# A chunked mLSTM mixer and its MLP on one core: the output gates get tiles of their own, F and g share one 128-row tile, w1's third rows are copied by DMA, and the plan has new numbers

## The chip, the core and the metric

The kernel runs on one core of a Trainium2 chip. Its metric is the device time in microseconds (us). Before the change the median of three runs is 384.98 us (384.32 to 384.99). The engines are TensorE (PE, its weight loads PEld), VectorE (DVE), ScalarE (ACT), GpSimd (POOL) and SyncE (SP), which issues nearly all DMAs.

## The reference

The first part is an mLSTM over 768 steps, for 4 batches of 8 heads of width 40; the second mixes the tokens of its output by a product of rank 32 and applies an MLP of width 320 to 1280 to 320.

```python
for t in range(S):                       # per batch and head
    m_new = max(f[t] + m, i[t])
    C = exp(f[t] + m - m_new) * C + exp(i[t] - m_new) * outer(v[t], k[t])
    n = exp(f[t] + m - m_new) * n + exp(i[t] - m_new) * k[t]
    m = m_new
    y[t] = sigmoid(o[t]) * (C @ q[t]) / max(abs(n . q[t]), 1.0)
x = y, heads side by side                # 4 x 768 x 320
u = x + (x^T @ U @ V)^T                  # mixes tokens
out = u + max(u @ w1, 0) @ w2
```

## The kernel before

The steps are cut into chunks of 128 tokens, three to a half (hf), two halves to a batch; the eight heads go in groups of 3, 3 and 2. For a half, the gates of all 32 batch-head rows are worked out at once (function gates): a running maximum (gate_max, L525), some differences, the running sum F of the log decays within a chunk (gate_sum, L534, the rows fs), and g = exp(F) (gate_exp). For each head, TensorE spreads F over 128 partitions (decay, function fbmm), ScalarE takes exp(F + a bias per token) in three pieces (decay_exp, L923), GpSimd masks the upper triangle (decay_mask, L926), VectorE multiplies with the scores of q and k (weigh, L937), and TensorE multiplies with V (pv). A group's state C is carried by kv, kv_mask and state; inter adds its part from q times g (q_decay, from g_rows for batch 0 and from a DMA for later batches). norm, out_norm and gate (L964 to L977) divide, multiply by the sigmoid of the output gate and write x. Batches 2 and 3 (from LOG_TO = 2) build the decays by a scan on VectorE (L933) from DMAs instead of exponentials on ScalarE.

TensorE's products in reduced form take each operand as a high part plus a low part (the names _high and _low): F and g are split so into the tiles fhl and ghl. fhl has four 32-row strips, F high, F low, F high, F low; a decay matmul uses 64 rows, so that two heads go as a pair on the two 64-row halves of the array. The weights come as 64-bit words, which ScalarE and VectorE turn into 32-bit floats (L649 to L654) and split; w1's third rows (64 of 320) are written to both halves of w1h's third strip (w13_high, L721).

The token tile tk of a group holds K, V and the output gates o of its three chunks. The sigmoid is taken in place (L773), for batches 0 and 1 three groups at a time (most = 3), for later ones singly. The sigmoid and the exponential use different tables of ScalarE.

The order of the work is not written by hand. Each operation is given to a planner (class Plan) with an engine or a choice of engines, a cost in ns, its reads and writes, the buffers it opens, and a priority: a due time plus a number from the table ORDER, by kind of operation and by half of a batch. The planner goes through simulated time, starts on each engine the ready operation of the smallest priority, and emits the instructions in this order; each engine's queue then runs in it, and so does SP's queue of DMAs. Operations that wait for a table of ScalarE's other than the one loaded get a penalty (SWITCH). PSUM's 8 banks are shared by the kinds st, at, m1, m2 and gt with a limit for each (SHARE). Where TensorE would be idle, or its use in a stretch of time too low, the planner emits fillers: matmuls of a zero tile into a free bank (keep_busy, warm). attention, mix and mlp give the planner the operations of a batch; the MLP of a half is 10 strips of up (eight matmuls of 384 columns each), relu and down (three times three matmuls of 320 columns).

Of the kernel before, what the change touches and what calls it, by code (L numbers as in the profile page):

```python
# [45 lines left out]
G_TO, QUAD_FROM = 1, 2  # L46
MASK_NS = 600.0
# [24 lines left out]
    "gate_w": (87.18, 86.38, 0.0, 0.0, 0.0, 0.0, 0.0, 0.0),
    "gate_exp": (96.46, 1090.3, 0.0, 0.0, 0.0, 0.0, 0.0, 0.0),
    "gate_w_exp": (82.17, 121.49, 0.0, 0.0, 0.0, 0.0, 0.0, 0.0),
    "store_g": (89.27, 82.16, 0.0, 0.0, 0.0, 0.0, 0.0, 0.0),
    "g_high": (823.51, 82.38, 0.0, 0.0, 0.0, 0.0, 0.0, 0.0),
    "g_low": (43.02, 90.34, 0.0, 0.0, 0.0, 0.0, 0.0, 0.0),
    "gate_f_exp": (44.34, 953.57, 0.0, 0.0, 0.0, 0.0, 0.0, 0.0),
    "gate_ends": (68.95, 85.66, 0.0, 0.0, 0.0, 0.0, 0.0, 0.0),
    "gate_i_exp": (72.57, 90.34, 0.0, 0.0, 0.0, 0.0, 0.0, 0.0),  # L80
    "store_decay": (67.79, 88.08, 0.0, 0.0, 0.0, 0.0, 0.0, 0.0),
    "gate_turn": (77.56, 86.18, 0.0, 0.0, 0.0, 0.0, 0.0, 0.0),
    "gate_keep": (75.92, 90.34, 0.0, 0.0, 0.0, 0.0, 0.0, 0.0),
    "gate_total": (44.17, 111.25, 0.0, 0.0, 0.0, 0.0, 0.0, 0.0),
    "totals": (66.83, 173.14, 0.0, 0.0, 0.0, 0.0, 0.0, 0.0),
    "totals_keep": (74.35, 104.22, 0.0, 0.0, 0.0, 0.0, 0.0, 0.0),
    "load_weights": (-8.4, 0.0, 0.0, 0.0, 0.0, 0.0, 0.0, 0.0),
# [1151 lines left out]
```

## Time and profile before

| | |
|---|---|
| profiled execution | 385.04 us |
| its span (first to last instruction) | 383.2 us |
| TensorE busy | 375.7 us, 98% |
| VectorE busy | 246.9 us, 64% |
| ScalarE busy | 164.8 us, 43% |
| GpSimd busy | 44.8 us, 12% |
| granted TensorE clock | 0.998 of 2.4 GHz |
| moved by DMA | 47.25 MB |

A share of the span is an average over stages that differ, and a matmul is counted as busy until its modelled end, which overlaps the next one's start: 12 matmuls that are listed at 285 ns each may hold the queue for under 1 us. What an operation holds of TensorE's queue is read from the start of the one behind it.

### The profile page before, as it was taken

To read this page: it belongs to the slowest core of one execution; us is meant where nothing else is said; L and a number is where in the kernel's file an instruction comes from. 1 tells how busy PE (TensorE), PEld (TensorE's weight loads), DVE (VectorE), ACT (ScalarE), POOL (GpSimd) and SP (SyncE) were. 2 spreads that over 40 slices of the span, in tenths; PEclk is the share of its full clock that TensorE was granted. 3 is DMA by queue.
4 is the path that set the end of the run, shared out by engine and by line. 5 is a ranking of instruction groups with operands and counts; after the bars stand their busy time and mean duration, and the time that the engine had idled before them with its cause. 6 is when DMAs were issued, how large, how long until landed. Compare 5 with 4: busy or idle time off the path is not lost.

```text
span 383.2 us, 7435 instructions
## 1 busy us (share of the span) xinstructions
PE 375.7 (98%) x2776; PEld 355.0 (93%) x2776; DVE 246.9 (64%) x562; ACT 164.8 (43%) x411; POOL 44.8 (12%) x68
## 2 busy tenths in 40 slices
PE   8999999999999999999999999999999999999996
PEld 6687877889999999999999999999999999999996
DVE  4977989989988857554498554888935334213222
ACT  6897697985976422132223142313222122213120
POOL 0123344223113300020010000002000000000000
PEclk9999999999999999999999999999999999999999
DMA  8958999576725732156276341553201000000001
GB/s 192 351 177 237 274 246 256 169 202 186 226 84 154 213 89 85 58 130 199 71 185 185 80 136 51 133 153 110 85 19 36 0 2 18 33 2 19 34 1 53
DMA packets 26052, 47.25 MB, mean 123 GB/s; under 512 B 4192, under 2 KB 17120, under 8 KB 26016
## 3 DMA queue, kind: packets, MB, share of 16 engines
q1 hardware_dynamic: 25824, 46.38, 42.2%
q8 instruction: 22, 0.36, 0.4%
q10 hardware_dynamic: 192, 0.40, 0.3%
q14 instruction: 14, 0.11, 0.1%
HBM read 41.85 MB, written 4.92 MB: 122 GB/s over the span
## 4 chain that ended last, share of the span: by engine, by line
PE 83%; DVE 7%; DMA 5%; ACT 2%; issue 2%; ACTq 0%; SPq 0%; DVEq 0%
PE ps L402 83%; DMA tk<-in_tk 2%; DMA q<-in_q 2%; DMA x<-in_fig 1%; DVE cv L654 1%; DVE cv L652 1%; DVE dm L937 1%; DVE w1l L699 0%; DVE w1l L723 0%; DVE fhl L546 0%; ACT dm L923 0%; DVE cv L650 0%; ACT L923 0%; ACT L1128 0%; ACT fhl L543 0%
## 5 line engine op out<-in xcount | busy, mean ns | idle before, releaser
L402 PE MATMUL ps<-w2h,h 128*128 128x320 f32 x480 | 118.8, 312 | 0.0
L402 PE MATMUL ps<-ut,w1h 128*128 128x384 f32 x400 | 117.9, 342 | 0.0
L1092 DVE SCALAR_TENSOR_TENSOR h<-ps,h 128x384 fp32r<-128x384 f32 x80 | 44.0, 552 | 77.1 <-ACT h L1090 76.8
L1090 ACT ACTIVATE h<-ps 128x384 fp32r<-128x384 f32 x80 | 39.0, 491 | 114.2 <-PE ps L402 114.2
L402 PEld LDWEIGHTS ps<-w2h,h 128*128 128x128 f32 x480 | 83.2, 188 | 0.7 <-issue 0.4
L402 PE MATMUL ps<-ut,w1l 128*128 128x384 f32 x240 | 80.6, 336 | 0.0
L402 PEld LDWEIGHTS ps<-ut,w1h 128*128 128x128 f32 x400 | 73.6, 188 | 1.4 <-issue 0.3
L402 PE MATMUL ps<-w2l,h 128*128 128x320 f32 x240 | 73.9, 308 | 0.0
L402 PE MATMUL ps<-tk,dm 128*128 128x82 f32 x384 | 49.9, 272 | 0.3 <-DVE dm L937 0.3
L402 PEld LDWEIGHTS ps<-tk,dm 128*128 128x128 f32 x384 | 47.3, 191 | 2.8 <-DVE dm L937 1.3
L402 PEld LDWEIGHTS ps<-ut,w1l 128*128 128x128 f32 x240 | 45.1, 188 | 0.0
L402 PEld LDWEIGHTS ps<-w2l,h 128*128 128x128 f32 x240 | 45.1, 188 | 0.0
L937 DVE TENSOR_TENSOR dm<-ps,dm 128x384 f32<-128x384 f32 x64 | 33.4, 545 | 5.2 <-PE ps L402 2.9
L933 DVE TENSOR_TENSOR_SCAN dm<-fd,ident 128x384 f32<-128x384 f32 x32 | 30.5, 960 | 5.1 <-DMA fd<-fsd 3.7
L923 ACT ACTIVATE dm<-ps,tok 128x128 f32<-128x128 f32 x96 | 26.9, 371 | 4.5 <-PE ps L402 4.4
L402 PE MATMUL ps<-qk 40*128 40x128 f32 x384 | 28.3, 285 | 0.0
L402 PEld LDWEIGHTS ps<-qk 40*128 40x128 f32 x384 | 23.6, 187 | 4.8 <-issue 3.3
L402 PE MATMUL ps<-zeros 128*128 128x256 bf16 x172 | 25.9, 294 | 2.0 <-DVE x L522 1.1
L926 POOL TENSOR_SCALAR_AFFINE_SELECT dm<-dm 128x384 f32<-128x384 f32 x32 | 18.9, 594 | 69.2 <-ACT dm L923 64.3
L402 PEld LDWEIGHTS <-zeros 128*128 128x128 bf16 x172 | 17.0, 106 | 6.8 <-issue 1.8
L1115 DVE TENSOR_TENSOR o<-ps,x 128x320 f32<-128x320 f32 x24 | 10.9, 487 | 9.9 <-PE ps L402 9.9
L402 PE MATMUL ps<-C,q 120*128 120x123 f32 (+1 forms) x120 | 17.2, 277 | 0.0
(101 smaller groups left out, 418.3 us busy)
## 6 DMA issues: line engine op xcount, KB each, us to landing
qk<-in_qk SPq DMA_DIRECT2D x64, 144.0 KB, 3.5
tk<-in_tk SPq DMA_DIRECT2D x16, 544.5 KB, 6.2
raw<-in_w SPq DMA_DIRECT2D x20, 320.0 KB, 4.1
fd<-fsd SPq DMA_DIRECT2D x32, 192.0 KB, 3.3
out<-o SPq DMA_DIRECT2D x24, 160.0 KB, 1.8
tk<-in_tk SPq DMA_DIRECT2D x8, 363.0 KB, 5.3
q<-in_q SPq DMA_DIRECT2D x16, 180.0 KB, 2.5
fd<-gsd SPq DMA_DIRECT2D x9, 120.0 KB, 3.8
```

What stands on the lines that cost most here:

```text
L402: nc.tensor.matmul(o, a, b, start=start, stop=stop, **kw)
L652: p.op("weight_sign" + at, pri, "dve", dve(n), lambda tu=tu, hi=hi: V.scalar_tensor_tensor(tu(), hi(), 0x80000000, tu(), ALU.bitwise_and, ...
L654: p.op("weight_tail" + at, pri, "dve", dve(n), lambda tu=tu, lo=lo: V.scalar_tensor_tensor(tu(), lo(), 29, tu(), ALU.logical_shift_right, ...
L923: nc.scalar.activation(T[kdm][:, cs], T[kfb][:, cs], AF.Exp, bias=tok[hf][:, 0, c, bh:bh + 1])
L926: p.op("decay_mask", at(u), "pool", MASK_NS, lambda kdm=kdm: nc.gpsimd.affine_select(out=T[kdm].rearrange("p (c t) -> p c t", t=P), in_=T[ ...
L933: lambda kfb=kfb, kdm=kdm: nc.vector.tensor_tensor_scan(T[kdm], T[kfb][:, 0:HS], ident3.rearrange("p c t -> p (c t)"), 0.0, ALU.mult, ALU. ...
L937: p.op("weigh", at(u), "dve", dve(HS), lambda ks=ks, kdm=kdm: nc.vector.tensor_mul(T[kdm], T[ks][:, 0:HS], T[kdm]), r=[ks], w=[kdm])
L1090: p.op("relu_high", pri + pace * m - 20.0, "act", 371, lambda: nc.scalar.activation(T[kh][:, 0, :], T[kp][:, 0:HS], AF.Relu), r=[kp], w=[( ...
L1092: p.op("relu_low", pri + pace * m - 20.0, "dve", dve(HS), lambda: nc.vector.scalar_tensor_tensor(T[kh][:, 1, :], T[kp][:, 0:HS], 0.0, f32( ...
L1115: p.op("residual", pri + 10 * pace - 20.0, "dve", dve(DM), lambda: nc.vector.tensor_add(T[ko], T[ka][:, 0:DM], T[X][:, tt, 0:DM]), r=[ka] ...
```

## The change

- The output gates leave the tile tk and get tiles ot of their own, eight of them; tk has 5 buffers instead of 6. A group is loaded by two DMAs (load_tk, load_o). The sigmoids of batches 0 and 1 are one operation of six groups (SIG_TO).
- fhl now has the strips F high, F low, g high, g low, and ghl is gone. The decay of one head is one matmul over 128 rows (idsel is zero where g stands), planned head by head with PSUM banks of a new kind dt (two at most); g_rows uses the lower two strips by gsel. High and low parts of F are written once. g itself is placed on partitions 64 to 95, and a small exponential (gate_end) makes the chunk ends for gate_total.
- w13_high writes one half of the strip, and a DMA from SBUF to SBUF (w13_copy) writes the other.
- load_gates1 goes from ScalarE's DMA queue to SP's; idents and the filling of gsel are two operations. Batch 1 takes its scores four heads at a time (QUAD_FROM). fd and cv have one buffer more.
- The planner's costs change a little (the mask 650 for 600, the first DMAs 300 later, rebase 30 more, three exponentials at 252 each for 264), and all numbers of ORDER are new.

```diff
-G_TO, QUAD_FROM = 1, 2
-MASK_NS = 600.0
+G_TO, QUAD_FROM, SIG_TO = 1, 1, 2
+MASK_NS = 650.0
...
-    "gate_max": (100.41, 117.37, 0.0, 0.0, 0.0, 0.0, 0.0, 0.0),
-    "gate_sum": (679.0, 84.04, 0.0, 0.0, 0.0, 0.0, 0.0, 0.0),
...
+    "load_gates1": (69.08, 0.0, 0.0, 0.0, 0.0, 0.0, 0.0, 0.0),
+    "gate_max": (11.11, 48.17, 0.0, 0.0, 0.0, 0.0, 0.0, 0.0),
+    "gate_sum": (14.44, 39.41, 0.0, 0.0, 0.0, 0.0, 0.0, 0.0),
...
-    "tk": (6, [P, 3 * 3 * (2 * D + DV)], F32),
+    "tk": (5, [P, 3 * 3 * (D + DV)], F32),
+    "ot": (8, [P, 3 * 3 * D], F32),
...
-    "fd": (3, [P, HS], F32),
+    "fd": (4, [P, HS], F32),
...
-    "cv": (3, [P, CW], F32),
+    "cv": (4, [P, CW], F32),
...
-SHARE = {"st": ("ps", 4), "at": ("ps", 4), "m1": ("ps", 3), "m2": ("ps", 3), "gt": ("ps", 2)}
+SHARE = {"st": ("ps", 4), "at": ("ps", 4), "m1": ("ps", 3), "m2": ("ps", 3), "gt": ("ps", 2), "dt": ("ps", 2)}
...
-        p.op("load_gates1", -98, "aq", dma(NBH * S * 4), lambda: nc.scalar.dma_start(out=xf(S, S), in_=fig[:, S:2 * S]), w=[(XF, "f", 1), (XF, "i", 1)])
+        p.op("load_gates1", -98, "sp", dma(NBH * S * 4), lambda: nc.sync.dma_start(out=xf(S, S), in_=fig[:, S:2 * S]), w=[(XF, "f", 1), (XF, "i", 1)])
...
-            g = lambda hf=hf: g1(2 * S + hf * HS, HS)
+            g = lambda hf=hf: T[G1].rearrange("p c d -> p (c d)")[2 * NBH:3 * NBH, hf * HS:(hf + 1) * HS]
+            gt = lambda hf=hf: g0(2 * S + 1 + 2 * B * 3 + 3 * hf, 3)
...
-            for n in range(2):
-                hi, lo = [slice((2 * n + i) * NBH, (2 * n + i + 1) * NBH) for i in range(2)]
-                p.op("decay_high", pr + n, "act", act(HS), lambda hf=hf, fs=fs, hi=hi: nc.scalar.copy(fhl[hf][hi, :], fs()), r=[kfs], w=[("fh", hf, n)])
-                p.op(
-                    "decay_low", pr + n, *both(HS),
-                    lambda e, hf=hf, fs=fs, lo=lo: e.tensor_sub(fhl[hf][lo, :], fs(), f32(fhl[hf][0:NBH, :])),
-                    r=[kfs, ("fh", hf, 0)], w=[("fhl", hf, n)],
-                )
+            p.op("decay_high", pr, "act", act(HS), lambda hf=hf, fs=fs: nc.scalar.copy(fhl[hf][0:NBH, :], fs()), r=[kfs], w=[("fh", hf)])
+            p.op("decay_low", pr, ("pool", "dve"), (pool(HS), 100 + dve(HS)), lambda e, hf=hf, fs=fs: e.tensor_sub(
+                fhl[hf][NBH:2 * NBH, :], fs(), f32(fhl[hf][0:NBH, :])), r=[kfs, ("fh", hf)], w=[("fl", hf)])
...
+            p.op("g_high", pr + 4, "act", act(HS), lambda hf=hf, g=g: nc.scalar.copy(fhl[hf][2 * NBH:3 * NBH, :], g()), r=[kg], w=[("ghl", hf, 0)])
+            p.op("g_low", pr + 4, ("pool", "dve"), (pool(HS), 100 + dve(HS)), lambda e, hf=hf, g=g: e.tensor_sub(
+                fhl[hf][3 * NBH:4 * NBH, :], g(), f32(fhl[hf][2 * NBH:3 * NBH, :])), r=[kg, ("ghl", hf, 0)], w=[("ghl", hf, 1)])
...
+            p.op("gate_end", pr, "act", 80, lambda fs=fs, gt=gt: nc.scalar.activation(gt(), fs()[:, P - 1::P], AF.Exp), r=[kfs], w=[(G0, "gt", hf)], table="exp")
...
-                for z in range(2):
-                    p.op("w13_high", pri + 20 * a, "act", act(CW), lambda rs=rs, fs=fs, z=z: nc.scalar.copy(
-                        w1h[64 * z:64 * z + 64, 2, fs], t()[rs]), r=[kc], w=[(kh, z)])
+                p.op("w13_high", pri + 2 * a, "act", 100 + act(CW), lambda rs=rs, fs=fs: nc.scalar.copy(
+                    w1h[rs, 2, fs], t()[rs]), r=[kc], w=[(kh, a)])
+                p.op("w13_copy", pri + 2 * a, "sp", dma(64 * CW * 4), lambda rs=rs, fs=fs, a=a: nc.sync.dma_start(
+                    out=f32(w1h[64 * (1 - a):64 * (2 - a), 2, fs]), in_=f32(w1h[rs, 2, fs])), r=[(kh, a)], w=[(kh, 1 - a)])
...
-            def load():
-                c0, cn = 3 * h0 * (2 * D + DV), 3 * nh * (2 * D + DV)
-                nc.sync.dma_start(out=T[kt][:, 0:cn], in_=tk[b, hf, :, c0:c0 + cn])
-
-            p.op("load_tk", at(n) - 8, "sp", dma(P * 3 * nh * 121 * 4), load, w=[(kt, "k"), (kt, "v"), (kt, "o")], new=[(kt, "tk")])
+            c0, cn = 3 * h0 * (2 * D + DV), 3 * nh * (D + DV)
+            p.op("load_tk", at(n) - 8, "sp", dma(P * cn * 4), lambda: nc.sync.dma_start(
+                out=T[kt][:, 0:cn], in_=tk[b, hf, :, c0:c0 + cn]), w=[(kt, "k"), (kt, "v")], new=[(kt, "tk")])
+            kot, co = ("ot", b, j), 3 * nh * D
+            p.op("load_o", at(n) - 4, "sp", dma(P * co * 4), lambda: nc.sync.dma_start(
+                out=T[kot][:, 0:co], in_=tk[b, hf, :, c0 + cn:c0 + cn + co]), w=[(kot, "o")], new=[(kot, "ot")])
...
-                mm(T[kgb][0:r, tg], gsel[:, h0 * D:h0 * D + r], ghl[hf][:, tg])
+                mm(T[kgb][0:r, tg], gsel[:, h0 * D:h0 * D + r], fhl[hf][:, tg])
...
-                if h % 2 == 0:
-                    fbs = [("fb", b, hf, h + i) for i in range(2)]
-
-                    def fbmm(fbs=fbs, bh=bh):
-                        for i, kfb in enumerate(fbs):
-                            rs = slice(64 * i, 64 * i + 64)
-                            mm(T[kfb][:, 0:HS], idsel[rs, bh + i:bh + i + 1].to_broadcast([64, P]), fhl[hf][rs, :], start=True, stop=True)
-
-                    if logs:
-                        p.op("decay", at(u), "pe", 173 + 190, fbmm,
-                             r=[("fh", hf, n) for n in range(2)] + [("fhl", hf, n) for n in range(2)] + [("idents",)],
-                             w=fbs, new=[(k, "at") for k in fbs], load=0.5)
+                def fbmm(kfb=kfb, bh=bh):
+                    mm(T[kfb][:, 0:HS], idsel[:, bh:bh + 1].to_broadcast([P, P]), fhl[hf])
+
+                if logs:
+                    p.op("decay", at(u), "pe", 180, fbmm, r=[("fh", hf), ("fl", hf), ("idents",)], w=[kfb], new=[(kfb, "dt")], load=0.9)
...
-        most = 3 if b < LOG_TO else 1
+        most = 6 if b < SIG_TO else 3 if b < LOG_TO else 1
...
-        nc.scalar.copy(ghl[hf][64:P, :], zeros[64:P, 0:1].to_broadcast([P - 64, HS]))
+        nc.scalar.copy(fhl[hf][2 * NBH:P, :], zeros[2 * NBH:P, 0:1].to_broadcast([2 * NBH, HS]))
+    nc.scalar.copy(idsel[2 * NBH:P, :], zeros[2 * NBH:P, 0:NBH])
```

The other lines follow from these: readers of o take it from ot, and the keys of fhl's strips are renamed.

## Rows read from the trace of the kernel before

**Rows 1.** Busy time of the engines by stretch: us, then busy (xinstructions), clock, DMA.

```profile
10.00:20.00 10.00, 9.03 (x79) 6.71 (x76) 9.70 (x24) 9.29 (x25) 2.69 (x3) 1.00 1.04 358
20.00:55.00 35.00, 34.27 (x306) 28.76 (x304) 28.61 (x77) 28.66 (x83) 11.92 (x20) 1.00 0.83 230
55.00:78.00 23.00, 21.81 (x168) 18.48 (x168) 22.81 (x56) 20.65 (x53) 7.29 (x10) 1.00 0.80 208
78.00:384.00 306.00, 301.70 (x2167) 294.31 (x2166) 180.86 (x400) 100.00 (x242) 22.19 (x30) 1.00 0.32 94
```

**Rows 2.** The chain that ended last: start, length, what.

```profile
39.00 9.53 DMA tk<-in_tk
...
78.06 183.15 PE ps L402 x1364
```

**Rows 3.** The same stretches, only instructions on the zero tile (fillers).

```profile
10.00:20.00 10.00, 4.78 (x38) 3.08 (x35) 0.00 (x0) 0.00 (x0) 1.00 1.04 358
20.00:55.00 35.00, 7.51 (x52) 4.70 (x52) 0.00 (x0) 0.00 (x0) 1.00 0.83 230
55.00:78.00 23.00, 4.85 (x32) 3.03 (x33) 0.00 (x0) 0.00 (x0) 1.00 0.80 208
```

**Rows 4.** Start in order of time: start, length, engine, line, operation [idle before].

```profile
7.65 1.01 DVE L525 TENSOR_TENSOR_SCAN x<-x,x 32x384 f32<-32x384 f32 x1 [1.24 <-DMA x<-in_fig]
...
7.90 3.01 PE L402 MATMUL ps<-zeros 128*128 128x256 bf16 x26
...
9.64 0.94 DVE L534 TENSOR_TENSOR_SCAN x<-x 32x384 f32<-32x384 f32 x1
...
10.61 1.03 ACT L543 CAST fhl<-x 32x384 fp32r<-32x384 f32 x2 [3.03 <-DVE x L534]
...
15.22 1.13 DVE L546 TENSOR_TENSOR fhl<-x,fhl 32x384 fp32r<-32x384 f32 x2
```

**Rows 5.** DMA issues: count, KB each, median us to landing.

```profile
tk<-in_tk SPq DMA_DIRECT2D x16, 544.5 KB, 6.2
raw<-in_w SPq DMA_DIRECT2D x20, 320.0 KB, 4.1
```

**Rows 6.** ScalarE's groups in 10 to 78 us.

```profile
L773 ACT ACT_TABLE_LOAD x4 | 5.1, 1283 | 0.1
...
L721 ACT CAST w1h<-cv 64x320 fp32r<-64x320 f32 x8 | 3.7, 460 | 0.7 <-DVE cv L654 0.6
```

**Rows 7.** ScalarE in order of time: a table load, third-row copies.

```profile
53.33 1.28 ACT L773 ACT_TABLE_LOAD   x1
54.63 1.19 ACT L773 ACTIVATE tk<-tk 128x360 f32<-128x360 f32 x3
...
67.25 1.88 ACT L721 CAST w1h<-cv 64x320 fp32r<-64x320 f32 x4 [0.61 <-DVE cv L654]
```

**Rows 8.** TensorE in order of time: decays, first matmuls on w1, scores of a pair.

```profile
43.30 0.94 PE L402 MATMUL ps<-qk 40*128 40x128 f32 x12
44.17 0.69 PE L402 MATMUL ps<-v,tk 128*120 128x123 f32 x4
...
70.96 0.44 PE L402 MATMUL ps<-fhl,idsel 64*128 64x384 f32 x2
71.33 0.44 PE L402 MATMUL ps<-ut,w1h 128*128 128x384 f32 x1
71.61 0.34 PE L402 MATMUL ps<-ut,w1l 128*128 128x384 f32 x1
71.78 0.34 PE L402 MATMUL ps<-ut,w1h 128*128 128x384 f32 x1
```

**Rows 9.** TensorE in order of time: scores of four heads.

```profile
189.70 1.61 PE L402 MATMUL ps<-qk 40*128 40x128 f32 x24
191.24 0.41 PE L402 MATMUL ps<-w2h,h 128*128 128x320 f32 x1
```

**Rows 10.** SP's own waits in 15 to 78 us: total, times, longest.

```profile
SPq L885 <- PE ps L402: 10.9, 9, 4.9
```

More of the change, by code (lines that the diff above doesn't have):

```diff
@@ L72 @@
[L72 to L87, printed above, removed]
@@ new lines @@
+    "gate_input": (-19.85, 44.13, 0.0, 0.0, 0.0, 0.0, 0.0, 0.0),
+    "idents": (70.0, 0.0, 0.0, 0.0, 0.0, 0.0, 0.0, 0.0),
+    "gsels": (55.38, 0.0, 0.0, 0.0, 0.0, 0.0, 0.0, 0.0),
+    "ident3": (-29.79, 0.0, 0.0, 0.0, 0.0, 0.0, 0.0, 0.0),
+    "decay_high": (-15.11, 42.84, 0.0, 0.0, 0.0, 0.0, 0.0, 0.0),
+    "decay_low": (-69.33, -35.13, 0.0, 0.0, 0.0, 0.0, 0.0, 0.0),
+    "gate_bias": (68.96, 72.39, 0.0, 0.0, 0.0, 0.0, 0.0, 0.0),
+    "gate_w": (-69.07, -57.24, 0.0, 0.0, 0.0, 0.0, 0.0, 0.0),
@@ new lines @@
+    "store_decay": (-50.54, 47.49, 0.0, 0.0, 0.0, 0.0, 0.0, 0.0),
+    "gate_turn": (52.91, -9.54, 0.0, 0.0, 0.0, 0.0, 0.0, 0.0),
+    "gate_keep": (46.28, 48.01, 0.0, 0.0, 0.0, 0.0, 0.0, 0.0),
+    "gate_end": (-17.92, 37.62, 0.0, 0.0, 0.0, 0.0, 0.0, 0.0),
+    "gate_total": (6.97, -41.77, 0.0, 0.0, 0.0, 0.0, 0.0, 0.0),
+    "totals": (0.01, 60.29, 0.0, 0.0, 0.0, 0.0, 0.0, 0.0),
+    "totals_keep": (-54.04, 56.19, 0.0, 0.0, 0.0, 0.0, 0.0, 0.0),
+    "load_weights": (-15.45, 0.0, 0.0, 0.0, 0.0, 0.0, 0.0, 0.0),
@@ new lines @@
+    "kv_mask": (-67.9, 39.86, -12.93, 58.65, -63.58, 22.9, 69.87, -7.22),
+    "state": (-69.31, 71.04, 67.84, -20.93, -43.52, 19.8, 20.59, -75.95),
+    "g_rows": (2.72, 70.0, 0.0, 0.0, 0.0, 0.0, 0.0, 0.0),
+    "q_decay": (-12.97, -25.03, 64.13, 51.4, 17.26, 4.24, 61.95, -22.43),
+    "load_qk": (-69.08, 60.41, 8.74, -48.12, 43.05, 68.3, 39.67, -70.0),
+    "scores": (19.6, -68.83, 39.35, -70.38, -42.77, -3.82, 57.55, -57.12),
+    "decay": (-47.23, -84.29, 0.09, -42.24, 0.0, 0.0, 0.0, 0.0),
@@ new lines @@
+    "gate": (-53.87, -16.25, -62.2, 33.77, 58.35, 24.98, 35.63, 45.28),
+    "again": (-21.37, -53.43, -4.69, -33.5, -61.33, 31.42, 49.2, -70.0),
+    "x_high": (0.0, -1.62, 0.0, 10.91, 0.0, -12.14, 0.0, 35.47),
+    "x_low": (0.0, -63.33, 0.0, -30.03, 0.0, 4.75, 0.0, 3.45),
+    "rows": (0.0, 60.85, 0.0, 19.25, 0.0, 66.38, 0.0, 57.55),
+    "rows_high": (0.0, 1.86, 0.0, 63.67, 0.0, -21.82, 0.0, 38.8),
+    "rows_low": (0.0, -53.85, 0.0, -0.02, 0.0, 35.58, 0.0, 64.7),
+    "rows_low2": (0.0, 0.98, 0.0, -3.05, 0.0, 30.57, 0.0, 70.0),
@@ L156 @@
+    "decay_scan": (0.0, 0.0, 0.0, 0.0, -70.0, -36.42, -33.48, 0.44),
 }
@@ L428, in mlstm_mixer_kernel @@
     fhl = [const.tile([4 * NBH, HS], F32R, name=f"fhl{hf}") for hf in range(2)]
-    ghl = [const.tile([P, HS], F32R, name=f"ghl{hf}") for hf in range(2)]
     gsel = const.tile([P, DM], F32R, name="gsel")
@@ L495, in idents, with gsels @@
         def idents():
-            for n in range(4):
+            for n in range(2):
                 ns = slice(n * NBH, (n + 1) * NBH)
                 nc.scalar.copy(idsel[ns, :], ident[ns, ns])
-            for n in range(2):
+        def gsels():
+            for n in range(2, 4):
                 nc.scalar.copy(gsel[n * NBH:n * NBH + NHEAD, :], cst[0:NHEAD, C_HSEL:C_HSEL + DM])
@@ L771, in ops @@
                     nh = GROUPS[js[j][0]][1]
-                    o = T["tk", b, j][:, 3 * nh * (D + DV):3 * nh * (2 * D + DV)]
+                    o = T["ot", b, j][:, 0:3 * nh * D]
                     nc.scalar.activation(o, o, AF.Sigmoid)
             p.op("sigmoid", at(n), "act", sum(act(3 * GROUPS[js[j][0]][1] * D) for j in range(j0, j1)), ops,
-                 w=[(("tk", b, j), "o") for j in range(j0, j1)], table="sig")
+                 w=[(("ot", b, j), "o") for j in range(j0, j1)], table="sig")
         def group(j, n):
@@ L856, in g_rows @@
             def g_rows():
-                mm(T[kgb][0:r, tg], gsel[:, h0 * D:h0 * D + r], ghl[hf][:, tg])
+                mm(T[kgb][0:r, tg], gsel[:, h0 * D:h0 * D + r], fhl[hf][:, tg])
             if b < G_TO:
-                p.op("g_rows", at(n), "pe", 175, g_rows, r=[("ghl", hf, 0), ("ghl", hf, 1), ("idents",)], w=[kgb], new=[(kgb, "gt")], load=0.9)
+                p.op("g_rows", at(n), "pe", 190, g_rows, r=[("ghl", hf, 0), ("ghl", hf, 1), ("fl", hf), ("gsel",)], w=[kgb], new=[(kgb, "gt")], load=0.9)
             else:
@@ L923, in decays @@
                             nc.scalar.activation(T[kdm][:, cs], T[kfb][:, cs], AF.Exp, bias=tok[hf][:, 0, c, bh:bh + 1])
-                    p.op("decay_exp", at(u), "act", 3 * 264, decays, r=[kfb, ("tok", hf, 0)], w=[kdm], new=[(kdm, "dm")], table="exp")
+                    p.op("decay_exp", at(u), "act", 3 * 252, decays, r=[kfb, ("tok", hf, 0)], w=[kdm], new=[(kdm, "dm")], table="exp")
                     p.op("decay_mask", at(u), "pool", MASK_NS, lambda kdm=kdm: nc.gpsimd.affine_select(
```

143 lines of the change are left out of this document (63 added, 80 removed), and 33 rows, old and new, of the table ORDER.

## The prediction

> **What bounds the kernel now.** Read first the table of busy time by stage [rows 1]. From 78 us to the end TensorE is busy 301.7 of the 305.2 us that are left, VectorE 180.9, ScalarE 100.0. The chain of waits agrees: from 78.06 us on it is one piece of TensorE after another [rows 2]. So behind 78 us only TensorE's own work counts. Ahead of it the picture is another: in 55 to 78 us VectorE is busy 22.81 of 23 us and ScalarE 20.65; in 20 to 55 us no engine but TensorE is full, and the DMA engines are at 0.83; in 10 to 20 us ScalarE (9.29) and VectorE (9.70) are both nearly full. TensorE looks full there too (0.90 to 0.98), but the same table for the zero tile [rows 3] says what with: 38, 52 and 32 of its matmuls in these three stretches are fillers (256 columns of a zero tile, which the planner puts in where the engine would be idle or lightly used). The granted clock is 1.00 in every stretch [rows 1], so the clock is not what the time hangs on.
>
> One filler holds the queue for about 0.11 us: 26 in a row took 3.01 us, the last one's 0.27 us being latency, (3.01 - 0.27) / 25 [rows 4]. So the 122 fillers of 10 to 78 us are 122 x 0.11 = 13.4 us, and TensorE's idle time there is 0.97 + 0.73 + 1.19 = 2.9 us [rows 1]. These 16.3 us are the pool from which any better order in the early part can be paid; nothing else is to be had but real work of TensorE itself.
>
> The profiled execution took 385.04 us for a span of 383.2 us; the median of the three runs is 384.98, so the sum is made against 385.0.
>
> **The start of the gates.** The first half's running sum (L534) starts at 9.64 us, behind the second half's running maximum (L525), for which VectorE idled 1.24 us until its gates landed at 7.65 [rows 4]. The sum's own input was ready before that: the operation ahead of the 1.24 us gap ended at 7.65 - 1.24 = 6.41 us. So the order alone costs up to 9.64 - 6.41 = 3.2 us, and ScalarE waits 3.03 us for it before the decays' high half [rows 4]. Behind it the low half was written twice, the last time from 15.22 us on [rows 4], and the first decay matmul needs both. The new numbers put the first half's sum ahead of the second half's maximum (-90 + 14.44 against -89 + 48.17, the smaller goes first), and one high and one low copy are left where there were two. The second half's gates go from ScalarE's queue to SP's, by their number (-98 + 69.08) behind the first six loads of q and k and two of q, so they land later; what needs them comes some microseconds later as well. Upper end of the gain: 5.2 us, all fillers (38 x 0.11 = 4.2) and idle time (0.97) of 10 to 20 us. Lower end 0: the first K and V tiles may land no sooner (6.2 us median for a token tile [rows 5]), and then the decays only wait for them. I take 3.2, since the matmuls that use the decays ran well behind the sum, and since the token tile gives up a third of its bytes (the output gates), so that its part lands sooner.
>
> **ScalarE: tables and copies.** In 10 to 78 us there are four table loads for the sigmoid, 1.283 us each, and a way back to the exponential's table for each of them, and eight copies of w1's third rows at 0.46 us [rows 6]. With six sigmoids in one bunch for batches 0 and 1, each of these batches needs one way there and back instead of two: 4 loads less, 5.1 us. Half of the eight third-row copies become DMAs: 1.8 us. Both are in the stretch 20 to 78 us but for the first moments: 6.9 of ScalarE's 49.3 busy us. The sigmoid loads of batches 2 and 3 stay single and fall behind 78 us, where ScalarE is two thirds idle: nothing. What do 6.9 us of ScalarE give? At most 6.9, if each ended a filler; at least nothing, as VectorE is the full engine in 55 to 78 us. The pool of 20 to 78 us is 84 fillers x 0.11 + 1.92 = 11.2 us, 19% of the stretch; 19% of 6.9 is 1.3, and with the mask multiplication that the planner may now give to ScalarE instead of VectorE I take 1.5.
>
> The Trainium skill ("ScalarE: Activation LUTs", What ACT_TABLE_LOAD costs) puts a drain of some 1.38 us on top of each load; then four loads would be worth 10.6 us and the term 2.4. The trace has no such time: the load at 53.33 us lasts 1.28, and the sigmoids start at 54.63 [rows 7].
>
> **Scores in fours for batch 1 (QUAD_FROM 1).** A pair of heads holds TensorE from 43.30 to 44.17, 0.87 us; four heads from 189.70 to 191.24, 1.54 us against 2 x 0.87 = 1.74 [rows 8, 9]. Batch 1 has 16 heads by halves, so four such groups: 4 x 0.2 = 0.8 us. This is work of TensorE and counts wherever it lies. Ends 0 (the four banks of scores come free later) and 0.8; I take 0.8.
>
> **Decay rows by 128 instead of 2 x 64 rows.** Now two matmuls of 64 rows go as a pair: 70.96 to 71.33, 0.37 us [rows 8]. Then there are two of 128 rows, one after the other. A matmul of the same 384 columns takes 0.17 us in a row of its like (71.61 to 71.78) and 0.28 us as the first of them (71.33 to 71.61). Both in a row of their like: 0.34, 16 pairs, -0.5 us. Each alone: 0.56, 16 x 0.19 = +3.0 us. One after the other: 0.45, 16 x 0.08 = +1.3. With two banks for decays they can often stand together: I take +1.0.
>
> The Trainium skill speaks against this part ("TensorEngine Tiling (Array Packing)", Key Properties): different tiles run their loads and matmuls in parallel, so a pair would cost one matmul's time, and taking it apart adds 0.17 us each, 2.7 us in all. The same list says that changing the tiling mode drains the engine, and the trace is with that: the pair's 0.37 us is twice 0.17, so the parallel run is paid back by the change of mode.
>
> **The rest at nothing.** The copy of idents, the zero fill of one tile instead of another, two tiny exponentials for the ends (gate_end), a split token load (the same bytes, 24 more issues), and one more buffer for fd and cv each. The work that hides them is the same as before; the exceptions are the third rival.
>
> The sum: -3.2 - 1.5 - 0.8 + 1.0 = -4.5, so 385.0 - 4.5 = 380.5 us. By the ends: all gains high 5.2 + 6.9 + 0.8 + 0.5 = 13.4 (371.6), all low +3.0 (388.0).
>
> **Rivals.** (A) ScalarE counts in full. VectorE's waits and the mask stage hang on ScalarE's decays, and the new buffers let weights run ahead. Then about half the pool of 16.3 us goes, 8.2, and the scores' 0.8 less the decays' 1.0: 377.0. For it: ScalarE is at 0.82 and 0.90 in 20 to 55 and 55 to 78 us. Against it: the pool shrinks least where VectorE is full.
>
> (B) VectorE and the weights set the end of the early part. VectorE is busy 61.1 of the 68 us between 10 and 78 us, and the change takes from it only two low copies (about 1.1 us). Attention is done sooner, but the first matmuls on w1 still start near 71 us [rows 8]; the fillers only move behind the attention work. What is left is the scores' 0.8, the two copies' 1.1, less 1.0: 384.1. For it: 55 to 78 us, where the chain runs through VectorE. Against it: what starts sooner gives VectorE work in its 6.9 idle us.
>
> (C) Slower: SP's queue is held. All loads go through it in order. Each split load and each copied third-row tile is one more entry that can wait for a buffer or for ScalarE, with all loads behind it. A held load of q and k waited up to 4.9 us, 10.9 in all of 15 to 78 us [rows 10]. The last four third-row copies ran at 67.25 to 69.13 [rows 7]; a DMA in their place lands 4.1 us (weights) to 9.53 us (the token load in the chain) after its issue [rows 2, 5], so for the second strip between 67.7 + 4.1 = 71.8 and 77.2. The third group of eight matmuls on w1 reads that strip; it comes 16 x 0.17 = 2.7 us behind 71.33, at 74.1 with the first one's 0.11 [rows 8], and holds TensorE's whole queue while it waits. One such copy late is up to 77.2 - 74.1 = 3.1 us; together with one hold of 4.9 us that reaches TensorE it is 8.0, against the 4.5 gained: 388.5. It decides from 4.5 us of waits that TensorE sees. Against it: copies can be issued earlier, as the third rows' numbers are now 2 apart instead of 20.
>
> (D) The pairs of 64 rows were worth more than the rows show, and the decay matmuls stand alone: +3.0 instead of +1.0, 382.5. For it: the first matmul of its kind held the queue for 0.28 us [rows 8]. Against it: two banks let two heads' decays follow each other. The Trainium skill's rule of parallel tiles ("TensorEngine Tiling (Array Packing)", Key Properties) would end near here too, with its 2.7 us in place of the 1.0: 382.2.
>
> **How the numbers follow.** Forecast 0.42 (378.5 to 382.5), A 0.20 (374 to 378.5), D 0.08, B 0.12, C 0.18. What a measurement here can tell from no change is 0.2%, 0.8 us. Faster: forecast, A and D, 0.70, and a third of B, 0.04: 0.74, of which I take 0.04 off for a plan whose 110 numbers all moved: 0.70. Same: most of B, and the edge of C: 0.10. Slower: C, and what was taken off: 0.20. The range from 374.5 to 386.5 leaves out most of C and the far end of A.
>
> **What would show it.** Right: L534 of the first half starts near 7 us, not 9.64; the first decay matmul before 13 us; four table loads less ahead of 78 us; fewer than 90 fillers in 10 to 78 us; four fewer changes of tiling mode by scores and none by decays; w1's first matmul before 69 us. Wrong: w1's matmuls wait for a DMA of w1h; the fillers are as many as before, only later; the single decay matmuls hold the queue 0.28 us each; TensorE shows idle time behind 78 us. The sum is wrong as a whole if the early order is worse than the one it replaces.

## The result, and the profile after

The changed kernel takes 381.07 us in the median of six runs, the kernel before 384.65 on the same chip; the ratio is 0.9906, with a 95% interval of 0.9891 to 0.9921. (One of the six, 392.62 us at a granted clock of 0.969, was disturbed; here and below such executions are left out of the ratios, but not out of the medians.) The forecast was 380.5 us. The profiled execution took 380.81 us for a span of 379.1; before, it was 383.2. So the spans differ by 4.1 us.

The first line of the page after, busy time by engine:

```profile
PE 368.4 (97%) x2741; PEld 353.1 (93%) x2741; DVE 242.5 (64%) x550; ACT 159.8 (42%) x415; POOL 50.7 (13%) x73
```

The stages after, as in [rows 1]:

```profile
10.00:20.00 10.00, 9.27 (x69) 7.50 (x69) 8.85 (x23) 8.65 (x31) 3.73 (x6) 1.00 1.07 341
20.00:55.00 35.00, 32.45 (x293) 28.46 (x291) 28.06 (x74) 26.00 (x83) 13.60 (x21) 1.00 0.96 265
55.00:78.00 23.00, 21.26 (x195) 19.45 (x195) 22.55 (x57) 21.64 (x54) 9.95 (x12) 1.00 0.84 239
78.00:384.00 306.00, 296.59 (x2131) 291.41 (x2129) 177.24 (x387) 95.52 (x235) 22.74 (x29) 1.00 0.32 90
```

And of these the zero tile (fillers), as in [rows 3]:

```profile
10.00:20.00 10.00, 2.91 (x21) 1.82 (x21) 0.00 (x0) 0.00 (x0) 1.00 1.07 341
20.00:55.00 35.00, 6.28 (x45) 4.07 (x45) 0.00 (x0) 0.00 (x0) 1.00 0.96 265
55.00:78.00 23.00, 4.96 (x36) 3.17 (x36) 0.00 (x0) 0.00 (x0) 1.00 0.84 239
```

Behind 78 us TensorE has 5.1 us less to do (296.59 against 301.70). Ahead of it the fillers fell most in 10 to 20 us, from 38 to 21, and 15 fewer start ahead of 10 us; in 20 to 78 us they are 81 where they were 84, and TensorE's idle time rose there from 1.92 to 4.29 us (58 less the busy time of the two stretches).

To weigh this, each matmul of both timelines was given the time from its start to the start of the next, less an idle time of over 0.15 us ahead of the next; the last one was given the time to the end of the span. The two sums then differ as the spans do:

| us | before | after | difference |
|---|---|---|---|
| fillers and idle, up to 20 us | 14.7 | 10.8 | -4.0 |
| fillers and idle, 20 to 78 us | 12.0 | 13.6 | +1.7 |
| fillers and idle, behind 78 us | 0.3 | 1.1 | +0.8 |
| all other matmuls | 356.2 | 353.6 | -2.6 |
| sum | 383.2 | 379.1 | -4.1 |

(The rows are rounded; a class of matmuls in such a sum is good to some 0.5 us, since a few records are missing.) So about half of the gain or more is TensorE's own work: scores -0.8, products with the decays (tk,dm) -1.5, the decay matmuls themselves +1.4, the rest -1.8.

The start, in order of time: the first half's sum (L541), ScalarE's high part (L549), the first decay matmuls, the second half's maximum (L532), which waits for its gates.

```profile
6.81 0.95 DVE L541 TENSOR_TENSOR_SCAN x<-x 32x384 f32<-32x384 f32 x1
8.45 0.49 ACT L549 CAST fhl<-x 32x384 fp32r<-32x384 f32 x1
...
10.75 0.59 PE L407 MATMUL ps<-fhl,idsel 128*128 128x384 f32 x2
...
11.05 1.00 DVE L532 TENSOR_TENSOR_SCAN x<-x,x 32x384 f32<-32x384 f32 x1 [0.89 <-DMA x<-in_fig]
```

The sum starts 2.83 us sooner than in [rows 4], the first decay matmul 5.0 us. In the kernel before it was this one:

```profile
15.78 0.48 PE L402 MATMUL ps<-fhl,idsel 64*128 64x384 f32 x2
```

ScalarE's table loads and third-row copies in 10 to 78 us, as in [rows 6]; three loads are for the sigmoid and three for the way back (there were four and four):

```profile
L779 ACT ACT_TABLE_LOAD x3 | 3.8, 1283 | 0.1
...
L922 ACT ACT_TABLE_LOAD x2 | 2.6, 1283 | 0.0
L724 ACT CAST w1h<-cv 64x320 fp32r<-64x320 f32 x4 | 1.9, 464 | 0.0
L574 ACT ACT_TABLE_LOAD x1 | 1.3, 1283 | 0.0
```

The lead is given back in two places. The first is near 52 us: in 50 to 55 us TensorE is busy 3.07 us only, the hole that runs 9 and 10 are about. The stretch, the chain and the timeline:

```profile
50.00:55.00 5.00, 3.07 (x26) 2.36 (x24) 3.54 (x10) 4.10 (x14) 1.90 (x3) 1.00 1.05 265
```

```profile
46.48 7.38 DMA q<-in_q
```

```profile
50.85 0.48 ACT L653 ACTIVATE cv<-raw 128x320 f32<-128x320 f32 x1 [1.22 <-DMA raw<-in_w]
51.24 2.42 ACT L922 ACTIVATE dm<-ps,tok 128x128 f32<-128x128 f32 x9
52.16 2.25 PE L407 MATMUL ps<-zeros 128*128 128x256 bf16 x19 [1.85 <-ACT dm L922]
54.49 0.90 PE L407 MATMUL ps<-C,q 80*128 80x82 f32 x6
```

TensorE stands for 1.85 us and then runs 19 fillers. The exponentials it waits for stand on ScalarE behind a weight that had not landed, and the state product behind the fillers needs a q that took 7.38 us to land. The DMA engines are full there, but they were so before as well (1.05 now and 0.98 before in 50 to 55 us, when TensorE was busy 4.97 us of the 5). What is new lies ahead: the share of 20 to 40 us went from 0.69 to 0.88, and in 20 to 55 us from 0.83 to 0.96. The second place is at 76 us:

```profile
72.01 0.42 PE L407 MATMUL ps<-ut,w1h 128*128 128x384 f32 x1
...
74.32 1.28 ACT L922 ACT_TABLE_LOAD   x1
75.62 0.88 ACT L922 ACTIVATE dm<-ps,tok 128x128 f32<-128x128 f32 x3
76.31 0.41 PE L407 MATMUL ps<-ut,w1h 128*128 128x384 f32 x1 [1.39 <-ACT dm L922]
```

The first matmul on w1 is 0.68 us later than in [rows 8], not sooner, and at 76.31 us TensorE has waited 1.39 us for exponentials that stand behind a table load.

### The profile page after: what moved, and what is told of

It reads as the page before. It is cut to its first block, busy times and chain, and to the rows that moved or that the text cites. A ratio compares the mean times of both kernels' runs of the same rounds, so it can differ in the third digit from the quotient of the medians.

```text
span 379.1 us, 7409 instructions
## 1 busy us (share of the span) xinstructions
PE 368.4 (97%) x2741; PEld 353.1 (93%) x2741; DVE 242.5 (64%) x550; ACT 159.8 (42%) x415; POOL 50.7 (13%) x73
## 4 chain that ended last, share of the span: by engine, by line
PE 86%; DVE 7%; DMA 4%; issue 1%; ACT 1%; SPq 1%; POOL 0%; DVEq 0%
PE ps L407 86%; DMA q<-in_q 3%; DVE C L849 1%; DMA qk<-in_qk 1%; DVE cv L656 0%; DVE dm L936 0%; DVE dm L932 0%; ACT dm L922 0%; DVE ot L971 0%; DVE w1l L703 0%; DVE q L869 0%; DVE w1l L728 0%; DVE x L541 0%; DVE cv L654 0%; DVE cv L658 0%
## 5 line engine op out<-in xcount | busy, mean ns | idle before, releaser
L407 PE MATMUL ps<-ut,w1h 128*128 128x384 f32 x400 | 120.0, 342 | 1.4 <-ACT dm L922 1.4
L407 PE MATMUL ps<-tk,dm 128*128 128x82 f32 x384 | 49.1, 270 | 0.5 <-DVE dm L936 0.5
L407 PE MATMUL ps<-qk 40*128 40x128 f32 x384 | 26.8, 283 | 0.0
L407 PE MATMUL ps<-zeros 128*128 128x256 bf16 x137 | 21.4, 302 | 5.0 <-ACT dm L922 2.4
L407 PEld LDWEIGHTS <-zeros 128*128 128x128 bf16 x137 | 13.7, 108 | 8.5 <-issue 2.8
```

Of the source, the lines that this page charges most:

```text
L407: nc.tensor.matmul(o, a, b, start=start, stop=stop, **kw)
```

## The experiments

In all but two of them the order in which the planner gave out the work was kept as it is, and changed only at the place named; so nothing else was planned anew. Each was timed in five rounds against the kernel before (medians 384.3 to 384.7). Differences in us between two of these kernels are differences of their ratios times 384.7, each ratio being uncertain by some 0.3%, 1.1 us, and such a difference by some 1.3 us.

**1. The start undone** (a_start_undone): in the changed kernel the first half's sum again behind the second half's maximum.

```diff
 VectorE: ...
+gate_max (second half)
 gate_sum (first half)
 ...
-gate_max (second half)
```

> The changed kernel, every queue in its order, but the second half's running maximum again ahead of the first half's running sum on VectorE. The sum then starts behind the second half's gates, which land at 11.05 us: near 12.0 instead of 6.8 us, some 5.2 us later. If the earlier start is what the change gained (theory), most of that comes back at the end: 384 to 386 us against 381.1. If VectorE and the loads of 20 to 78 us decide and take a lead away again (rival), it costs under 1 us: 381 to 382.

Measured: 387.56 us, ratio 1.0055 (1.002 to 1.0089), 5.7 us more than the change and beyond what either theory expected. TensorE's wait and the stretches:

```profile
13.57 0.53 PE L588 MATMUL ps<-cst,x 32*128 32x32 f32 x3 [4.38 <-DVE x L554]
```

```profile
15.00:20.00 5.00, 5.00 (x24) 3.30 (x23) 2.86 (x9) 3.68 (x13) 1.12 (x2) 0.50 1.03 340
20.00:25.00 5.00, 4.88 (x22) 4.11 (x21) 2.83 (x6) 2.66 (x11) 1.59 (x3) 0.50 0.70 185
25.00:30.00 5.00, 5.00 (x39) 5.00 (x39) 4.50 (x12) 4.56 (x15) 2.74 (x4) 0.86 0.56 149
```

The sum started at 12.02 us, since the second half's gates land later in this kernel. Products on TensorE wait for what VectorE makes of the sum. The fillers of the old order were not put back, so TensorE was idle for 4.38 us, and the granted clock then was 0.50, which is 1.2 GHz, until past 25 us. The run says that the order and the fillers belong together; the start's own price has to be read with a running engine (run 3).

**2. The start alone** (b_start_alone): in the kernel before, the first half's sum and what follows it ahead of the second half's maximum.

```diff
 VectorE, ScalarE: ...
+gate_first, gate_sum, decay_high, gate_bias, gate_w, decay_low x2 (first half)
 gate_max (second half)
 ...
```

> The kernel before, every queue in its order, but the first half's sum, bias, weights and both low copies on VectorE ahead of the second half's maximum. The sum starts near 6.4 instead of 9.64 us, the first decay matmul near 13 instead of 15.8. Theory (the start pays by itself): 2 to 3 us less than the kernel before, 381.5 to 382.7. Rival (the order behind it is made for the late start, and absorbs a lead): 384.2 to 384.7.

Measured: 383.69 us, ratio 0.999 (0.9954 to 1.0027): no difference that can be told. Both low parts were done by 9.91 us, and still the first decay matmuls came at 15.61:

```profile
8.80 1.11 DVE L548 TENSOR_TENSOR fhl<-x,fhl 32x384 fp32r<-32x384 f32 x2
```

```profile
8.30 3.01 PE L404 MATMUL ps<-zeros 128*128 128x256 bf16 x26
...
15.61 0.44 PE L404 MATMUL ps<-fhl,idsel 64*128 64x384 f32 x2
```

TensorE's queue still had its 26 fillers and the rest of the old order ahead of them. A sooner input was worth nothing here, where the reader's own queue kept its order.

**3. The start late, TensorE kept busy** (e_start_late_bridged): in the changed kernel, idle work on VectorE ahead of the first sum, and 28 fillers more on TensorE. The added fillers overwrite a bank that is in use, so the values are not the reference's: this kernel is for its time alone.

```diff
+VectorE: 1 memset, 7 products of a spare tile
 VectorE: gate_sum (first half)
+TensorE: 28 fillers
 TensorE: gate_turn (first half)
```

> The changed kernel, every queue in its order, with some 3.2 us of idle work on VectorE ahead of the first half's running sum (one memset and seven multiplications of a spare tile), and 28 more fillers ahead of TensorE's first transposes of the gates, so that TensorE does not stand still while it waits (the run before this one stood still for 4.4 us and fell to a granted clock of 0.5). So the whole start is 3.2 us late at full clock. If a lead at the start reaches the end (theory, as in the prediction), 383.5 to 384.3 us against 381.1. If the stage of 20 to 78 us absorbs it (rival), 381 to 382.

Measured: 383.88 us, ratio 0.9974 (0.9949 to 0.9998), 2.6 us more than the change (1.5 to 3.7 by the intervals). The sum starts at 10.36 instead of 6.81:

```profile
6.79 3.65 DVE L1176 TENSOR_TENSOR o<-o 128x320 f32<-128x320 f32 x7
10.36 0.94 DVE L543 TENSOR_TENSOR_SCAN x<-x 32x384 f32<-32x384 f32 x1
...
13.76 0.62 PE L409 MATMUL ps<-fhl,idsel 128*128 128x384 f32 x2 [0.34 <-DVE fhl L571]
```

The granted clock stays at 1.00. A delay of 3.55 us takes 2.6 us back, so about three quarters of it reach the end. This is the price of the first step of the sum, as near as it was measured: the sum is 3.55 us later, where the change had brought it 2.83 us forward, and the first decay matmul 3.0 us later, where the change had brought it 5.0 us forward.

**4. The decays alone** (c_decay_alone): in the kernel before, each pair of 64-row decay matmuls becomes two of 128 rows (the lower half of the selecting tile is zero, so the products are the same).

```diff
-mm(T[kfb][:, 0:HS], idsel[rs, ...].to_broadcast([64, P]), fhl[hf][rs, :], ...)
+mm(T[kfb][:, 0:HS], idsel[:, ...].to_broadcast([P, P]), fhl[hf])
```

> The kernel before, every queue in its order, but each pair of 64-row decay matmuls is two 128-row ones (the lower half of the selecting tile is zero, the output is the same). By the prediction's rows +1.0 us (0 to +3.0): 385.6 against 384.65. If the two 64-row tiles really ran in parallel and the change of tiling mode cost nothing, +2.7: 387.3. If the change of mode costs more than the rows showed (it is charged to the instruction behind the pair as well), a gain of 1 us or more: 383.6 or less.

Measured: 383.59 us, ratio 0.996 (0.9929 to 0.9991): 1.5 us faster by the ratio, 1.1 by the medians, where +1.0 had been forecast. One pair in the kernel before, with its neighbours:

```profile
32.10 0.88 PE L402 MATMUL ps<-tk,dm 128*128 128x82 f32 x6
32.91 0.44 PE L402 MATMUL ps<-fhl,idsel 64*128 64x384 f32 x2
33.28 0.90 PE L402 MATMUL ps<-tk,dm 128*128 128x82 f32 x6
34.02 0.64 PE L402 MATMUL ps<-C,q 120*128 120x123 f32 x4
```

And in this run:

```profile
31.92 0.88 PE L404 MATMUL ps<-tk,dm 128*128 128x82 f32 x6
32.59 0.59 PE L404 MATMUL ps<-fhl,idsel 128*128 128x384 f32 x2
33.03 0.79 PE L404 MATMUL ps<-tk,dm 128*128 128x82 f32 x6
33.66 0.64 PE L404 MATMUL ps<-C,q 120*128 120x123 f32 x4
```

From start to start the decays hold 0.44 us instead of 0.37, as forecast (0.45). But the six products ahead of them hold 0.67 instead of 0.81, and the six behind 0.63 instead of 0.74: in sum 1.74 instead of 1.92. The pair's price stood in its neighbours' rows. Over all 16 pairs of the two traces such sequences (the row ahead, the pair, the row behind) hold 1.6 us less in sum, about what the kernel gained. They are not all alike, from 0.33 us less to 0.24 us more: twice, behind 12 scores of 40 rows, the scores ahead hold 0.87 instead of 0.69 us, and the step costs time. The rows carry the tile shape with them (64*128 for the pair, 128*128 for its neighbours here). The Trainium skill says that the engine is drained when the tiling mode changes ("TensorEngine Tiling (Array Packing)", Key Properties). The trace agrees as far as it goes; if it is this drain, the 0.14 and 0.11 us are its size at this place.

**5. No DMA for w1's third rows** (d_no_copy_dma): ScalarE writes the second half again.

```diff
-nc.sync.dma_start(out=f32(w1h[64 * (1 - a):64 * (2 - a), 2, fs]), in_=f32(w1h[rs, 2, fs]))
+nc.scalar.copy(w1h[64 * (1 - a):64 * (2 - a), 2, fs], f32(w1h[rs, 2, fs]))
```

> The changed kernel, every queue in its order, but the second half of w1's third strip is written by ScalarE (four copies of 0.46 us more) instead of by a DMA. Theory: the DMAs hid and ScalarE has room, so no difference beyond 0.5 us: 380.6 to 381.6. If the copies by DMA hold SP's queue or w1's matmuls (rival C of the prediction), it is 1 us or more faster. If ScalarE counts in full (rival A), it is 1 to 1.8 us slower.

Measured: 381.69 us, ratio 0.9918 (0.9886 to 0.9949), 0.5 us more than the change: no difference that can be told. Four copies on ScalarE, or four DMAs that land in 4.7 us, are both hidden.

**6. A batch's bunch split** (h_bunch_split): the six sigmoids of batch 0 as three and three again.

```diff
-sigmoid (batch 0, groups 0 to 5)
+sigmoid (batch 0, groups 0 to 2)
 ... exponentials, totals_keep
+sigmoid (batch 0, groups 3 to 5)
```

> The changed kernel, every queue in its order, but batch 0's six sigmoids are three at their place (near 24 us) and three behind the exponentials of the second half's first heads (near 34 us), as in the kernel before: two more table loads, 2.6 us of ScalarE, at 34 to 37 us, where ScalarE is busy 3.5 to 3.9 of 5 us. By the prediction's 19% of ScalarE's time: +0.5 us, 381.6. If bunching is where the gain comes from: +1.5 to 2.6 us. If ScalarE has room: no difference.

Measured: 382.11 us, ratio 0.9927 (0.9899 to 0.9956): 0.8 us more, which is within the uncertainty of all that was expected, from nothing to 1.5 us and more. Eight table loads are in 10 to 78 us again instead of six.

**7. The lone sigmoid later** (f_sigmoid_later): batch 2's sigmoid of 72.7 us, which takes a table load and a way back for itself, beside the one at 83 us.

```diff
-sigmoid (batch 2, third)
 ...
+sigmoid (batch 2, third)
 sigmoid (batch 2, second half, first)
```

> The changed kernel, every queue in its order, but one sigmoid of batch 2, for which ScalarE loads its table at 71.40 us and the exponential's again at 74.32, is put next to the following sigmoid of batch 2 (near 83 us): two table loads less, 2.6 us of ScalarE, where TensorE stands 1.39 us for ScalarE's exponentials. If these two loads cause that stand (theory), 1 to 1.5 us faster: 379.6 to 380.1. If VectorE is the bound there all the same (rival), under 0.5 us.

Measured: 381.24 us, ratio 0.9907 (0.9878 to 0.9936): no difference that can be told. The two table loads are gone, and TensorE waits as before, now for VectorE:

```profile
77.62 0.41 PE L409 MATMUL ps<-ut,w1h 128*128 128x384 f32 x1 [1.71 <-DVE x L978]
```

**8. Both queues relieved there** (m_sigmoid_later_gate_first): as run 7, and batch 2's gate ahead of two subtractions of w1's low part on VectorE, two more of them on GpSimd.

```diff
 VectorE: ...
-w13_low, w_low, w_low, w_low
 norm, out_norm, gate (batch 2)
+w_low, w_low
+GpSimd: w13_low, w_low
```

> The changed kernel with batch 2's sigmoid of 71 us beside the one of 83 us (as in the run where only that was moved, 381.24), and on VectorE the gate of batch 2's second group ahead of two subtractions of w1's low part, while two more of these subtractions go to GpSimd, which stands idle from 72 to 74 us. Theory, that the wait near 76 to 78 us changes its engine only because VectorE's queue is next in line: the gate at L976 comes some 1.5 to 2 us earlier, TensorE's wait of 1.4 to 1.7 us shrinks below 0.5, and 1.0 to 1.5 us come off the end: 379.5 to 380.3. Rival, that the matmuls of w1 behind it then wait for the low parts or for w1's strips, which come later (DMA, ScalarE's rebase at 78): the wait moves again and the time stays at 380.8 to 381.5.

Measured: 380.61 us, ratio 0.9893 (0.9861 to 0.9924), the lowest median of all, 0.5 us below the change but not apart from it. The wait itself is closed: in 75 to 80 us TensorE is busy 4.79 us instead of 3.69. The stretch in the changed kernel, then in this run, and the wait that follows:

```profile
75.00:80.00 5.00, 3.69 (x23) 3.73 (x24) 5.00 (x14) 4.64 (x15) 1.58 (x4) 1.00 0.87 243
```

```profile
75.00:80.00 5.00, 4.79 (x37) 4.17 (x38) 5.00 (x13) 3.52 (x14) 1.50 (x3) 1.00 0.78 232
```

```profile
82.33 0.27 PE L409 MATMUL ps<-zeros 128*128 128x256 bf16 x1 [0.96 <-DVE h L1093]
```

The wait for the same line that follows grows from 0.64 us (at 83 us in the changed kernel) to 0.96 and takes part of it back: in 70 to 85 us TensorE is busy 0.8 us more. The theory was right about the place; the time lies between the ranges of theory and rival and decides for neither.

**9. The output gates later, with their sigmoids** (g_gates_later): six loads of batch 1's output gates from 20 to 51 us moved to 53, their sigmoids beside batch 2's at 62.

```diff
-load_o (batch 1) x6
 ...
+load_o (batch 1) x6
 w13_copy
 ...
+sigmoid (batch 1)
 sigmoid (batch 2)
```

> The changed kernel, every queue in its order, but the six loads of batch 1's output gates stand behind the loads of the first weights on SP's queue (near 53 us instead of 17 to 51 us), and their six sigmoids next to batch 2's first ones (62 us instead of 57.5). In 40 to 55 us the DMA engines are at 1.05 and TensorE is busy only 3.07 of 5 us in 50 to 55 us, waiting for exponentials behind a weight load and for q. If the early output gates take that bandwidth (theory: the split load hurts by what it brings too soon), 1 to 2 us faster: 379 to 380. If not (rival: the weights and q are late by themselves), no difference: 380.6 to 381.6.

Measured: 383.72 us, ratio 0.9979 (0.9953 to 1.0006), 2.8 us more than the change and beyond what either theory expected. The stretches, then ScalarE's bunch and TensorE's wait:

```profile
50.00:55.00 5.00, 4.63 (x46) 3.80 (x47) 4.97 (x12) 4.39 (x16) 3.71 (x5) 1.00 0.95 312
...
65.00:70.00 5.00, 3.54 (x31) 2.75 (x29) 2.56 (x8) 4.96 (x14) 0.92 (x2) 0.83 0.85 245
70.00:75.00 5.00, 5.00 (x24) 4.85 (x22) 4.38 (x9) 4.28 (x9) 2.23 (x4) 0.50 0.79 191
```

```profile
62.01 3.06 ACT L781 ACTIVATE ot<-ot 128x360 f32<-128x360 f32 x8
...
68.02 1.43 PE L409 MATMUL ps<-qk 40*128 40x128 f32 x10 [1.44 <-ACT dm L924]
```

The hole of 50 to 55 us closes (TensorE 4.63 us busy; it was 3.07), as it does in run 10, so these loads at their early place did open it. But the bunch of eight sigmoids and the table load behind it hold the exponentials back, TensorE waits 1.44 us for them in 65 to 70 us, and the granted clock falls to 0.50, which is 1.2 GHz.

**10. The gates later, the sigmoids in place** (l_gates_behind_q): only the five early loads move, to 50 us, behind the q that was late.

```diff
-load_o (batch 1) x5
 ...
 load_q (batch 2), w1's strips, load_tk
+load_o (batch 1) x5
 load_o (batch 1), the sixth
```

> The changed kernel with the five early loads of batch 1's output gates (issued between 20 and 39 us) moved on SP's queue to about 50 us, beside the sixth, behind the second q load of batch 2 and the fourth set of w1's strips; the sigmoids stay where they are. Theory, that these loads ahead of q and raw are what opens the hole of 50 to 55 us (TensorE 3.07 of 5 us busy, ScalarE and TensorE waiting for raw and q): the hole closes to over 4.2 us busy and, as the sigmoids are not moved, 0.8 to 1.8 us come off the end: 379 to 380.5. Rival, that the DMA engines are full from 5 to 60 us and the loads only change places: the sigmoids at 57 us then wait for the gates, exponentials of batch 2 come later, and the time is 381 to 384.

Measured: 381.93 us, ratio 0.9931 (0.9909 to 0.9953), no better than the change. The stretches, what is late on ScalarE in the second of them, and TensorE's wait:

```profile
50.00:55.00 5.00, 4.63 (x43) 3.67 (x43) 4.97 (x12) 4.93 (x18) 3.49 (x5) 1.00 1.05 334
...
65.00:70.00 5.00, 3.73 (x42) 3.24 (x40) 3.82 (x9) 3.42 (x11) 1.81 (x3) 1.00 0.95 273
```

```profile
66.90 0.49 ACT L655 ACTIVATE cv<-raw 128x320 f32<-128x320 f32 x1 [1.50 <-DMA raw<-in_w]
...
68.51 0.44 PE L409 MATMUL ps<-vst,pst 128*128 128x384 f32 x1 [1.27 <-DVE pst L1009]
```

The hole closes and another opens 15 us later, where a weight lands late. The DMA engines are at 1.00 and above from 50 to 65 us: what one load gains, another seems to lose. The time is the rival's.

**11 and 12. Old structure with new numbers, new structure with old numbers** (i_before_new_numbers, j_after_old_numbers): planned anew, with the tables ORDER exchanged.

```diff
-ORDER = {its own}
+ORDER = {the other kernel's}
```

> The kernel before in structure (gates inside tk, pairs of 64-row decays, no copy by DMA, three sigmoids a load), with the changed kernel's planner numbers for the 85 or so kinds that both have. Theory, that the numbers were found for the changed structure and carry only the order of the start: the first half's sum comes first as in the changed kernel and the first decay matmuls start before 13 us, worth about 2.6 us, but the rest of the order fits this structure badly: 384 to 392, not below 383. Rival, that the numbers do it all and the structure nothing: 380 to 382.

> The changed kernel's structure with the planner numbers of the kernel before (the four kinds that only it has keep theirs). Theory, that the structure alone brings the cheaper decays (1.1 to 1.5 us) and one table pair (0.8 us), but the old order of the start takes its 2.6 us back and the rest of the order is unfit: 383 to 391, at or above the kernel before. Rival, that the structure does it all: 380 to 382.

Measured: 408.14 us, ratio 1.0538 (1.0498 to 1.0579), and 406.19 us, ratio 1.0558 (1.0521 to 1.0594), both far beyond the ranges (the ratios stand for 405.0 and 405.8 us). The zero tile behind 78 us, old structure first, then new:

```profile
78.00:410.00 332.00, 16.16 (x115) 10.13 (x115) 0.00 (x0) 0.00 (x0) 1.00 0.31 91
```

```profile
78.00:410.00 332.00, 17.75 (x133) 11.90 (x130) 0.00 (x0) 0.00 (x0) 1.00 0.31 89
```

Behind 78 us, where both kernels have almost no fillers, there are now 115 and 133, some 13 to 15 us at 0.11 each. In the second the granted clock is 0.80 on average over 20 to 55 us as well. In both trials a table of numbers was far worse with the other structure than with its own, so the change can't be split into structure and plan by exchanging them.

## Why the prediction was right, and where it was not

The time was met (380.5 forecast, 381.07 measured), but two terms were off, one each way, and nearly cancelled. On the measure of the table, the part up to 20 us gave 4.0 us (3.2 forecast); 20 to 78 us lost 1.7 where a gain of 1.5 was forecast, and 0.8 more was lost behind it; TensorE's own work gave 2.6 where scores and decays together were to cost 0.2. That the sum came within 0.6 us is partly luck.

**The start, -3.2: right.** The sum's place on VectorE, together with TensorE's own order, did set the first decays (run 2: the sum's place alone did not move them), and run 3 prices it at 2.6 us. By 20 us TensorE had spent 4.0 us less on fillers and idling.

**ScalarE, -1.5: not borne out.** Four table loads were to go ahead of 78 us and two went, because the plan put one lone sigmoid of batch 2 there; the forecast had placed them all behind. (Two more went behind 78 us.) The runs price one pair of loads at 0.8 us (run 6), a second pair at nothing (run 7) and the copies at 0.5 us (run 5), each uncertain by 1.3, so they don't settle whether the price by the pool's average share of 19% was wrong. What is clear is that the pool of 20 to 78 us did not shrink, as the term has it, but grew by 1.7 us. One step that the forecast put at nothing has a part in this: the split token load. With the output gates apart, the plan loads those of batch 1 early, and these loads open the hole near 52 us (runs 9 and 10). TensorE waits there in a few places, and behind each stand two or three queues of nearly the same length: at 76 us ScalarE, then VectorE (runs 7 and 8), at 52 us the DMA engines, which runs 9 and 10 could only make late elsewhere. This is the share that rival B argued for. Rival A, half the pool gone, fails: by the forecast's own measure the pool of 10 to 78 us is 16.2 us (102 fillers at 0.11 and 5.0 idle) where it was 16.3.

**Scores in fours, -0.8: as forecast.** The scores hold 0.8 us less, and there are 20 groups of them where there were 24. No run takes this step alone, and the figure is good to some 0.5 us.

**Decays, +1.0: wrong in sign.** The two decay matmuls by themselves are as forecast where they stand as a pair: 0.44 us in run 4 (0.45 forecast). In the changed kernel many stand alone, and the 32 hold 8.3 us instead of 6.9, 0.26 us each, near the 0.28 that was named as a sign against. What failed is the step that priced the pair by its own time alone: the rows that were not read are those on either side, and the 64-row pair lengthened them. The 0.28 us of the first matmul on w1 in [rows 8], put down to its being the first of its kind, stood behind such a pair; in run 4 it is 0.18 at the next such place (82 us), though still 0.28 at 70 us. Alone, the step gives 1.1 to 1.5 us. Rival D, the same step priced still dearer, falls with it. Rival C does too: TensorE waits for no copy of w1h, and SP's queue waited 3.5 us in all for TensorE before loads of q and k, where it was 10.9.

**The signs.** Met: the sum near 7 us (6.81), the first decay before 13 us (10.75), four changes of tiling mode less by scores and none by decays (all 32 are of 128*128 now). Not met: fewer than 90 fillers in 10 to 78 us (102), four table loads less (two), w1's first matmul before 69 us (72.01). TensorE's idle time behind 78 us, named as a sign against, is 1.1 us on the measure of the table. That w1 started no sooner did not stop the gain: attention work that stood behind 78 us before stands ahead of it now (behind it there are 18 products with decays and 12 scores fewer).

What stays open: how the -1.8 us of the other matmuls comes about, what ScalarE's freed time is worth, and whether run 8 beats the change (0.5 us lower, at an uncertainty of 1.3).

## What to carry to other kernels

Price a change of a matmul's shape by a whole sequence, from the start of the neighbour ahead to the end of the one behind, in a place where the other shape stands too. Where three engines and the DMAs are all nearly full, relieving one may only move a wait by a few us (runs 7, 9 and 10): count only what the second queue at that wait leaves. And a table of priorities may suit one structure alone: exchanged, it cost some 20 us here, far more than any step of the change.
